# Holding all later zero fills of the GpSimd queue behind the FFN loads, and 42 instead of 50 up front

## Chip, cores, metric

One core of one Trainium2 chip. The metric is the device time of one execution in microseconds. All runs quoted here were fast. Ratios are computed as the mean time of one kernel's fast runs over that of the other's of the same rounds on the same chip, so they are not quite the ratios of the medians quoted beside them.

## The reference

A decode step (one token) of a transformer block: layernorm, attention of 16 query heads over 8 cached key and value heads, layernorm, a gated bilinear FFN; then all gradients of it. Only the last 4096 of the 32768 cache positions take part, so of the gradients of the two caches 7/8 are zero, and they must be written all the same:

```python
W = min(4096, max(256, Sk // 4))                       # 4096 of Sk = 32768
k = jnp.repeat(k_cache[:, :, Sk - W:, :], rep, axis=1)
v = jnp.repeat(v_cache[:, :, Sk - W:, :], rep, axis=1)
...
h2 = h + _B_ref(_layernorm(h), B_w_gate, B_w_up, B_w_down)
_out, _vjp = jax.vjp(_f, A_x, A_k_cache, A_v_cache, A_wq, A_wo, B_w_gate, B_w_up, B_w_down)
_grads = _vjp(grad_out)        # gradients of both caches: (1, 8, 32768, 256), bf16
```

## The kernel before

The zeros are written by 112 DMA transfers ("fills") of 2 MB each, all from one zeroed SBUF region, in rows of 16 KB (128 partitions x 8192 bf16). They are spread over three places: the GpSimd queue takes most, the SyncE queue takes 3 at each of five points around the FFN, and the last `NLATE` run on SyncE after everything else.

```python
ZW = 8192
NPRE = 50
NLATE = 9
fills = [zero_rows(o, g, 0, NZ, ZW)[i] for g in range(G) for o in (out_2, out_3) for i in range(NZ)]

def fill(eng, n):
    for _ in range(n):
        last = tc.keep_in_program_order(eng.dma_start(out=fills.pop(0), in_=zeros))
    return last

fill(ZQ, NPRE)                     # ZQ = GpSimd queue: the fills "up front"
# [... attention over 8 cache heads; their K and V are loaded on SyncE and ScalarE queues ...]
            elif g == 6:
                load_kv(V_at[7], A_v_cache, 7)
                load_wo(27, 32)
                fill(LD, 3)        # LD = SyncE queue
        load_wo(0, 19)
        load_ffn(*FB[0])
        fill(LD, 3)
# [... FFN, four rounds over the weights ...]
        for q, (f0, nw) in enumerate(FB):
            if q:
                load_ffn(f0, nw)   # w_down, w_gate, w_up; rows of 1 KB in w_gate and w_up
                fill(LD, 3)
            # [... compute; the next round's loads reuse this round's buffers ...]
        rest = fills[:-NLATE]
        for i, f in enumerate(rest):
            ins = ZQ.dma_start(out=f, in_=zeros)
            if i == 0:
                tc.add_manual_dep(ins.ins ..., ffn_last[0].ins.name, ..., reason="loads first")
# [... backward: 8 heads; each stores 2 x 2 MB through 3 staging buffers, and most also
#      weight-gradient "jobs" through 2 buffers, all on the SyncE queue ...]
            for o_ap, st_ in ((out_3, stV), (out_2, stK)):
                LD.dma_start(out=o_ap[0, g, Sk - W:, :].rearrange("(p t) d -> p t d", t=T), in_=st_)
            for job in plan[it]:
                job()
        for f in fills[-NLATE:]:
            tc.keep_in_program_order(LD.dma_start(out=f, in_=zeros))
```

Only the first fill of `rest` waits for the FFN loads, and without `keep_in_program_order` the scheduler may put the others in front of it.

Of the kernel before, what the change touches and what calls it, by code (L numbers as in the profile page):

```python
# [25 lines left out]
SCALE = 1.0 / 16.0  # L26
ZW = 8192
NZ = (Sk - W) * Dh // (128 * ZW)
NPRE = 50
NLATE = 9  # L30
KB = 512

# [2 lines left out]
def kernel(  # L35
# [5 lines left out]
    ZQ = nc.gpsimd  # L41
# [13 lines left out]
    def ar(off, n):  # L55
        return arena[:, off:off + n]
# [4 lines left out]
    zeros = ar(0, ZW)  # L61
# [67 lines left out]
    def fill(eng, n):  # L129
        last = None  # L130
# [4 lines that stand above are left out]
    fill(ZQ, NPRE)  # L135

# [244 lines left out]
    with tc.tile_pool(name="ps_mid", bufs=2, space=bass.MemoryType.PSUM) as ps_mid, \  # L381
# [61 lines left out]

        rest = fills[:-NLATE]
        for i, f in enumerate(rest):
            ins = ZQ.dma_start(out=f, in_=zeros)  # L446
            if i == 0:
                tc.add_manual_dep(ins.ins if hasattr(ins, "ins") else ins, ffn_last[0].ins.name, mybir.DependencyInfo(mybir.DependencyClass.Sync, mybir.DependencyReason.DATA), reason="loads first")

# [256 lines left out]
```

## Time and profile before

| | before |
|---|---|
| median of 4 runs | 838.37 us (837.80 to 838.44) |
| span of the profiled run | 836.3 us |
| bytes moved by DMA | 332.74 MB, 783 us at 425 GB/s |
| PE, VectorE, ScalarE busy | 55%, 44%, 24% |

The page of the kernel before has the busy tenths of the DMA engines and the rate they moved, in 40 slices of 20.9 us, and the DMA queues (q0 is the GpSimd queue, q1 SyncE, q10 ScalarE; packets, MB, share of the engines):

```profile
DMA  9999999999999999999999999999999987644699
GB/s 347 430 431 428 430 428 429 425 428 423 422 428 421 429 416 428 424 429 427 429 418 403 397 428 419 421 420 423 422 425 407 424 343 332 277 201 201 288 426 389
...
q0 software_dynamic: 12672, 184.56, 52.3%
q1 hardware_dynamic: 14758, 132.44, 38.1%
```

The DMA engines are full for 32 slices, then come six slices of a hole, then the nine late fills alone. A kernel bound like this can be read as a sum: the bytes at 425 GB/s, plus what the engines miss. The windows view of before, 20 us each (busy us of each engine with instruction counts, granted TensorE clock, DMA share, GB/s), shows the hole; it is 44 us of missed DMA. VectorE is the busiest compute engine in it:

```profile
core 0: us, PE busy (x) PEld busy (x) DVE busy (x) ACT busy (x) POOL busy (x), PEclk, DMA share, GB/s
660.00:680.00 20.00, 13.51 (x84) 6.00 (x83) 14.58 (x18) 7.43 (x12) 0.00 (x0) 0.69 1.00 423
680.00:700.00 20.00, 8.68 (x48) 4.02 (x49) 16.24 (x28) 6.24 (x11) 0.00 (x0) 0.66 0.76 302
...
740.00:760.00 20.00, 5.81 (x41) 1.85 (x41) 13.13 (x28) 9.26 (x17) 0.00 (x0) 0.52 0.47 197
...
780.00:800.00 20.00, 0.00 (x0) 0.00 (x0) 0.20 (x1) 0.03 (x1) 0.00 (x0) 0.50 0.99 419
```

The timeline of the GpSimd engine in before (start, duration, line; in brackets the idle time before it and what ended it) shows that the hold was not one. L132 is `fill`, L446 the loop over `rest`. Nine of these slip out before the held one goes at 468.63 us:

```profile
306.36 0.53 POOL L132 DMA_DIRECT2D out_dram<-arena  x1 [9.15 <-DMA out_dram<-arena]
312.66 0.53 POOL L446 DMA_DIRECT2D out_dram<-arena  x1 [5.78 <-DMA out_dram<-arena]
...
374.43 0.53 POOL L446 DMA_DIRECT2D out_dram<-arena  x1 [4.67 <-DMA out_dram<-arena]
468.63 4.18 POOL L446 DMA_DIRECT2D out_dram<-arena  x8 [93.68 <-DMA arena<-in_B_w_up_dram]
```

The chain of waits of before (start, duration, what) has the price of that: the first two FFN rounds wait 43 and 29 us for w_gate, the last two 10. A DMA piece of the chain runs from the issue of the transfer to its landing, so the engine behind it may have waited less (the waits view has 59.7 us of PE waiting for w_gate in all). The later lines are in the backward pass: VectorE, at the product of a weight-gradient job (L533), waits until one of the two job buffers is stored:

```profile
335.39 42.85 DMA arena<-in_B_w_gate_dram
...
402.70 28.73 DMA arena<-in_B_w_gate_dram
...
439.75 10.05 DMA arena<-in_B_w_gate_dram
...
457.52 9.71 DMA arena<-in_B_w_gate_dram
...
565.95 30.07 DMA out_dram<-arena
...
606.69 28.73 DMA out_dram<-arena
...
642.47 41.27 DMA out_dram<-arena
```

### The profile page before, as it was taken

To read this page: it belongs to the slowest core of one execution; us is meant where nothing else is said; L and a number is where in the kernel's file an instruction comes from. 1 tells how busy PE (TensorE), PEld (TensorE's weight loads), DVE (VectorE), ACT (ScalarE), POOL (GpSimd) and SP (SyncE) were. 2 spreads that over 40 slices of the span, in tenths; PEclk is the share of its full clock that TensorE was granted. 3 is DMA by queue.
4 is the path that set the end of the run, shared out by engine and by line. 5 is a ranking of instruction groups with operands and counts; after the bars stand their busy time and mean duration, and the time that the engine had idled before them with its cause. 6 is when DMAs were issued, how large, how long until landed. Compare 5 with 4: busy or idle time off the path is not lost.

```text
span 836.3 us, 8603 instructions
## 1 busy us (share of the span) xinstructions
PE 461.8 (55%) x3193; PEld 248.7 (30%) x3193; DVE 371.5 (44%) x1243; ACT 198.5 (24%) x325; POOL 51.9 (6%) x97
## 2 busy tenths in 40 slices
PE   0739999999994929041122319984534466542000
PEld 0414554554551505021011208542212232210000
DVE  2018256346240614020325490595746659965200
ACT  0322313323312000000000101572423143454100
POOL 4000010010010100010000201110000000000000
PEclk9969999999997969565555558996757666675555
DMA  9999999999999999999999999999999987644699
GB/s 347 430 431 428 430 428 429 425 428 423 422 428 421 429 416 428 424 429 427 429 418 403 397 428 419 421 420 423 422 425 407 424 343 332 277 201 201 288 426 389
DMA packets 28623, 332.74 MB, mean 398 GB/s; under 512 B 2979, under 2 KB 7206, under 8 KB 8742
## 3 DMA queue, kind: packets, MB, share of 16 engines
q0 software_dynamic: 12672, 184.56, 52.3%
q1 hardware_dynamic: 14758, 132.44, 38.1%
q10 hardware_dynamic: 1152, 15.20, 4.3%
q8 instruction: 25, 0.41, 0.2%
q14 instruction: 16, 0.13, 0.0%
HBM read 51.59 MB, written 280.59 MB: 397 GB/s over the span
## 4 chain that ended last, share of the span: by engine, by line
PE 39%; DMA 31%; DVE 13%; ACT 4%; another core or an unknown queue 4%; issue 1%; SPq 0%; DVEq 0%; ACTq 0%
DMA out_dram<-arena 13%; PE M_ps L334 13%; DMA arena<-in_B_w_gate_dram 11%; PE ok_ps L338 7%; PE rows_ps L274 7%; PE tr_ps L271 4%; DMA arena<-in_A_v_cache_dram 4%; DMA arena<-in_A_wq_dram 3%; DVE arena L649 3%; ACT arena L289 3%; DVE arena L650 2%; DVE arena L474 2%; PE d_ps L642 2%; PE dqb_ps L517 2%
## 5 line engine op out<-in xcount | busy, mean ns | idle before, releaser
L330 DVE TENSOR_SCALAR arena<-arena,p_f 128x256 bf16<-128x256 bf16 x512 | 110.0, 281 | 94.4 <-PE M_ps L334 94.4
L334 PE MATMUL M_ps<-arena 128*128 128x512 bf16 x512 | 125.3, 388 | 27.5 <-DMA arena<-in_A_v_cache_dram 27.5
L271 PE MATMUL tr_ps<-ident_bf,arena 128*128 128x128 bf16 x1024 | 90.5, 238 | 55.1 <-DMA arena<-in_A_k_cache_dram 31.0
L274 PE MATMUL rows_ps<-arena,vpad 128*16 128x512 bf16 x256 | 87.1, 438 | 30.2 <-DVE arena L606 22.0
L271 PEld LDWEIGHTS <-arena 128*128 128x128 bf16 x1024 | 67.7, 106 | 102.1 <-issue 50.9
L289 ACT COPY arena<-tr_ps 128x1024 bf16<-128x1024 bf16 x64 | 61.8, 1015 | 125.1 <-PE tr_ps L271 125.1
L642 PE MATMUL d_ps<-arena,rT 32*128 32x512 bf16 x256 | 40.2, 505 | 78.0 <-DVE arena L650 38.8
L334 PEld LDWEIGHTS <-arena 128*128 128x128 bf16 x512 | 46.9, 100 | 81.1 <-DMA arena<-in_A_v_cache_dram 28.0
L338 PE MATMUL ok_ps<-arena 128*16 128x256 bf16 x512 | 57.4, 273 | 0.9 <-DVE arena L316 0.9
L646 ACT CAST arena<-d_ps 128x512 bf16<-128x512 f32 x64 | 37.7, 590 | 67.5 <-PE d_ps L642 66.8
L650 DVE CAST arena<-d_ps 128x512 bf16<-128x512 f32 x64 | 43.5, 680 | 21.5 <-DMA out_dram<-arena 21.4
L649 DVE CAST arena<-d_ps 128x512 bf16<-128x512 f32 x64 | 43.9, 685 | 19.4 <-PE d_ps L642 19.3
L647 ACT CAST arena<-d_ps 128x512 bf16<-128x512 f32 x64 | 38.2, 596 | 48.7 <-DMA out_dram<-arena 48.7
L338 PEld LDWEIGHTS <-arena 128*16 128x16 bf16 x512 | 45.4, 90 | 13.9 <-issue 3.4
L423 PE MATMUL gu_ps<-X_b,arena 128*128 128x1 bf16 x84 | 7.2, 179 | 73.2 <-DMA arena<-in_B_w_gate_dram 59.7
L132 POOL DMA_DIRECT2D out_dram<-arena x50 | 27.1, 543 | 274.6 <-DMA out_dram<-arena 274.6
L604 ACT COPY arena<-tr_ps 128x1024 bf16<-128x1024 bf16 x32 | 32.7, 1021 | 42.2 <-DVE doX_f L474 23.5
L642 PEld LDWEIGHTS <-rT 32*128 32x128 bf16 x256 | 10.2, 95 | 100.4 <-issue 53.3
L274 PEld LDWEIGHTS <-vpad 128*16 128x16 bf16 x256 | 19.1, 91 | 64.2 <-issue 50.6
L446 POOL DMA_DIRECT2D out_dram<-arena x38 | 20.2, 532 | 282.4 <-DMA out_dram<-arena 188.8
L193 ACT CAST arena<-bc_ps 128x256 bf16<-128x256 f32 (+1 forms) x32 | 11.1, 347 | 107.1 <-PE bc_ps L192 105.9
L416 DVE CUSTOM_DVE_ANT_0 arena<-arena,dh_bc 128x448 bf16<-128x448 bf16 x14 | 8.8, 625 | 61.2 <-DMA arena<-in_B_w_down_dram 60.8
(193 smaller groups left out, 403.4 us busy)
## 6 DMA issues: line engine op xcount, KB each, us to landing
out_dram<-arena POOLq DMA_DIRECT2D x88, 2048.0 KB, 50.7
out_dram<-arena SPq DMA_DIRECT2D x40, 2048.0 KB, 19.9
arena<-in_A_k_cache_dram SPq DMA_DIRECT2D x7, 2048.0 KB, 15.1
arena<-in_A_v_cache_dram ACTq DMA_DIRECT2D x6, 2048.0 KB, 31.8
arena<-in_A_wq_dram SPq DMA_DIRECT2D x2, 3072.0 KB, 23.7
arena<-in_A_v_cache_dram SPq DMA_DIRECT2D x3, 2048.0 KB, 15.9
out_dram<-arena SPq DMA_DIRECT2D x3, 1344.0 KB, 22.1
out_dram<-arena SPq DMA_DIRECT2D x3, 1024.0 KB, 12.6
```

What stands on the lines that cost most here:

```text
L271: nc.tensor.transpose(tr_ps[:, dh, i, :], X_sb[:, 4 * q + i, dh * 128:(dh + 1) * 128], ident_bf[:])
L274: nc.tensor.matmul(rows_ps[:], lhsT=pad[:, dh, 16 * q:16 * q + 16], rhs=XT[:, dh].rearrange("p t k -> p (t k)"), start=(q == 0 and dh == 0 ...
L289: sT_ps = dots(K_at[g], KT_slot, vpad[g % 2], rows1, ps_c, "cols", lambda q, XT, ps: nc.scalar.copy(out=XT, in_=ps))
L330: nc.vector.tensor_scalar(out=pK[:, i, hh, :], in0=K_sb[:, t, :], scalar1=p_f[:, 8 * i + c, hh:hh + 1], scalar2=None, op0=ALU.mult)
L334: nc.tensor.matmul(M_ps[vh][:], lhsT=V_sb[:, t, vh * 128:(vh + 1) * 128], rhs=pK[:, i, :, :].rearrange("p h d -> p (h d)"), start=(t == 0) ...
L338: nc.tensor.matmul(ok_ps[:, k, :], lhsT=ppad[g % 2][:, 8 * (t % 4) + t // 4, :], rhs=X_sb[:, t, :], start=(g == 0 and k == 0 and t == 0), ...
L604: nc.scalar.copy(out=XT, in_=ps)
L642: nc.tensor.matmul(d_ps[:, qi].rearrange("p w d -> p (w d)"), lhsT=rT[32 * q:32 * (q + 1), :], rhs=RB_[32 * q:32 * (q + 1), l, :], start=T ...
L646: nc.scalar.copy(out=stV[:, t:t + 2, :], in_=d_ps[:, :, 0, :])
L647: nc.scalar.copy(out=stK[:, t:t + 2, :], in_=d_ps[:, :, 1, :])
L649: nc.vector.tensor_copy(out=stV[:, t:t + 2, :], in_=d_ps[:, :, 0, :])
L650: nc.vector.tensor_copy(out=stK[:, t:t + 2, :], in_=d_ps[:, :, 1, :])
```

## The change

The intent: clear the way for the FFN loads, and put the displaced fills where the hole is.

```diff
-NPRE = 50
+NPRE = 42
...
         for i, f in enumerate(rest):
-            ins = ZQ.dma_start(out=f, in_=zeros)
+            ins = tc.keep_in_program_order(ZQ.dma_start(out=f, in_=zeros))
             if i == 0:
                 tc.add_manual_dep(ins.ins ..., ffn_last[0].ins.name, ..., reason="loads first")
```

42 fills now go out up front and 46 stand behind the last FFN load.

## The prediction

> **What bounds the kernel now.** The DMA engines. The page: 332.74 MB, DMA digits 9 in the first 32 of 40 slices. In the table of 20 us windows they move 392 to 432 GB/s from 20 to 680 us, then only 302, 281, 197, 197 and 210 until 780, then about 425 for the nine zero fills that close the kernel. At 425 GB/s the bytes alone need 783 us. The hole from 680 to 780 us lacks 18.8 MB, 44 us; 783 + 44 + start and end give the span of 836. So only the hole, or new holes, can change the time. The Trainium skill (DMA: Bandwidth & Descriptors, Issuing engines are not separate DMA queues) says all queues share 16 engines; the trace agrees: GpSimd fills follow each other every 5 us alone, every 10 us beside SyncE transfers.
>
> **What the change does.** No work is added or removed; the other engines' instruction order stays. In before GpSimd issues 50 fills, and its timeline shows 9 more slip out from 313 to 374 us, ahead of the one held to 468.6 us; 29 follow there. After: 42, then 46 behind the last FFN load. 17 fills of 2.1 MB (35.7 MB, 84 us of DMA) move behind the FFN loads.
>
> **By stage.**
> 1. To about 306 us: the same (the 42nd fill lands there). V7's load, 15.9 us in the chain, gains 1 or 2 us.
> 2. About 308 to 332: only three SyncE fills are queued (15 us), PE still needs 24 us after V7 (chain). A new DMA gap of about 9 us.
> 3. FFN: the chain shows waits for w_gate of 42.9, 28.7, 10.1 and 9.7 us; the first two run beside GpSimd fills. The skill (same page, Queues, rings and completion order) says the engines switch between queues by packet, so small-row loads lose against 16 KB rows; the fills at full 5 us pace between 352 and 374 us, while the loads crawl, agree. Without fills all rounds take the 17 to 18 us of the last two (7.7 MB with three SyncE fills). The last FFN load should land near 397 us (380 to 410), not 468.6.
> 4. Backward: starts some 70 us earlier, its first cache-gradient stores at about 491, not 562. By then 16 of 46 fills are done, as in before. The other 30 (63 MB) share with 51.5 MB of SyncE traffic. In before such sharing (562 to 684) gave SyncE 201 GB/s and 37 to 53 us per head, against 20 to 25 without fills. Now it lasts for nearly all heads: last stores about 750 us, GpSimd fills to 755 to 775. The hole is mostly filled.
>
> Of 71 us gained in the FFN, most is given back by store waits. Balance: 836 - 44 (hole) + 9 (new gap) + 4 (FFN loops, DMA not quite full) + 3 (rest of a hole) = 808 span; the time runs 2 us longer.
>
> **Prediction: 810 us, range 797 to 827.** Faster by over 2%: 0.80; within 2%: 0.17; slower by over 2%: 0.03.
>
> **What would show it right.** GpSimd fills: 42, silence from about 260 to 397, then 46. First w_gate wait under 15 us, all FFN rounds near 18 us. DMA dips at 320 to 335 us. Store waits of 25 us or more until about 750 us; no window under 300 GB/s between 600 and 780. Matmul and VectorE busy times unchanged.
>
> **What would make it wrong.** FFN rounds limited by something else than bytes; fills draining well before the last heads, leaving a hole of 20 us or more; SyncE stores getting much less than half beside the fills, so that heads end after the fills and a compute tail remains; V7's load late.

## The result, and the profile after

The changed kernel took 828.31 us (median of 4 runs, 827.65 to 831.49), the kernel before 838.37: ratio 0.9889, 95% interval 0.9863 to 0.9915. It is 1.1% faster, where 3.4% was predicted, and lies just outside the stated range. The profiled run (831.49 us, span 829.7) was the slowest of the four, so its profile shows some 3 us more than the median.

The page of the changed kernel, same lines:

```profile
DMA  9999999999999994989999999999999999984799
GB/s 352 424 434 429 430 430 422 423 429 421 427 429 424 427 389 162 394 339 393 423 430 427 423 422 426 422 423 405 420 426 429 420 431 427 429 370 203 299 422 391
...
q0 software_dynamic: 12672, 184.56, 52.6%
q1 hardware_dynamic: 14758, 132.44, 38.7%
```

There is a new gap in the 16th slice and around it, and the late hole is shorter but not gone. The GpSimd timeline of the changed kernel shows the hold at work, and its chain of waits shows short FFN waits and a long series of store waits (the four below end again at weight-gradient jobs; four more, of 18, 17, 14 and 6 us, end at the copies into staging buffers):

```profile
260.47 0.53 POOL L132 DMA_DIRECT2D out_dram<-arena  x1 [8.62 <-DMA out_dram<-arena]
403.12 4.19 POOL L446 DMA_DIRECT2D out_dram<-arena  x8 [142.12 <-DMA arena<-in_B_w_up_dram]
```

```profile
391.51 10.21 DMA arena<-in_B_w_gate_dram
...
499.44 30.34 DMA out_dram<-arena
...
554.77 68.98 DMA out_dram<-arena x2
624.39 23.16 DMA out_dram<-arena
...
648.96 43.18 DMA out_dram<-arena
```

The last FFN load is in at 403 us instead of 469, 66 us sooner. But the last head's stores are issued at 774.06 us instead of 780.65. So 59 of the 66 us are handed back in the backward pass. The waits view says to whom; first the line of before, then that of the changed kernel (ScalarE at the copy into a staging buffer, waiting for its store: us in total, times, longest):

```profile
ACT arena L647 <- DMA out_dram<-arena: 48.7, 7, 13.5
```

```profile
ACT arena L647 <- DMA out_dram<-arena: 95.0, 7, 32.6
```

VectorE's waits for stores grew too: at its copy into a staging buffer (L650) from 21.4 to 50.7 us, at the weight-gradient products (L533) from 18.4 to 42.2. These waits overlap, so they don't add up.

### Why the store waits are long

The DMA view, limited to a window, counts packets and bytes by queue. One window of before, in which the FFN loads crawled (360 to 380 us):

```profile
q0 software_dynamic: 553, 8.03, 93.9%
q1 hardware_dynamic: 550, 0.53, 7.6%
```

The two queues moved the same number of packets, and 15 times the bytes went to the one with the long rows. The same two lines of the changed kernel, first at 535 to 555 us, where SyncE has mostly wide stores, then at 610 to 640 us, where the rows of out_8, of 3.5 and 1.8 KB, are among them:

```profile
q0 software_dynamic: 329, 4.72, 56.2%
q1 hardware_dynamic: 336, 3.77, 44.7%
```

```profile
q0 software_dynamic: 705, 10.26, 80.0%
q1 hardware_dynamic: 700, 2.53, 20.6%
```

In the second window, with packet counts equal again, SyncE has 2.53 MB in 30 us, 84 GB/s, and the stores of the heads queue behind its short rows.

A packet here is a row: 88 fills of 128 rows are 11,264, and 16 more for each fill make the 12,672 of q0 exactly. What these 16 are, no run here shows.

The Trainium skill (DMA: Bandwidth & Descriptors, Queues, rings and completion order) says that each engine takes turns between the queues packet by packet. The trace agrees, with 553 to 550, 705 to 700. So **while SyncE always has something to send and fills are there, each SyncE packet lets one fill packet pass.** The bytes of the rows, not a fair half, set the share.

### The profile page after: what moved, and what is told of

Its sections match the earlier page's. It is cut to its first block, busy times and chain, and to the rows that moved or that the text cites. A ratio compares the mean times of both kernels' runs of the same rounds, so it can differ in the third digit from the quotient of the medians.

```text
span 829.7 us, 8603 instructions
## 1 busy us (share of the span) xinstructions
PE 465.8 (56%) x3193; PEld 250.0 (30%) x3193; DVE 372.3 (45%) x1243; ACT 198.5 (24%) x325; POOL 53.0 (6%) x97
## 3 DMA queue, kind: packets, MB, share of 16 engines
q0 software_dynamic: 12672, 184.56, 52.6%
## 4 chain that ended last, share of the span: by engine, by line
PE 38%; DMA 37%; DVE 11%; ACT 4%; another core or an unknown queue 2%; issue 1%; SPq 0%; DVEq 0%; ACTq 0%
DMA out_dram<-arena 27%; PE M_ps L334 13%; PE ok_ps L338 7%; PE rows_ps L274 5%; PE tr_ps L271 4%; DMA arena<-in_A_v_cache_dram 3%; DMA arena<-in_A_wq_dram 3%; ACT arena L289 3%; DVE arena L649 2%; DVE arena L474 2%; PE dqb_ps L517 2%; DVE arena L650 2%; DMA arena<-in_B_w_down_dram 2%; PE d_ps L642 1%; DMA arena<-in_B_w_gate_dram 1%
## 5 line engine op out<-in xcount | busy, mean ns | idle before, releaser
L642 PE MATMUL d_ps<-arena,rT 32*128 32x512 bf16 x256 | 42.4, 519 | 115.9 <-ACT arena L647 68.6
L650 DVE CAST arena<-d_ps 128x512 bf16<-128x512 f32 x64 | 43.6, 682 | 50.7 <-DMA out_dram<-arena 50.7
L649 DVE CAST arena<-d_ps 128x512 bf16<-128x512 f32 x64 | 44.0, 687 | 21.4 <-PE d_ps L642 21.1
L276 DVE COPY arena<-rows_ps 16x512 f32<-16x512 f32 x16 | 10.8, 676 | 30.0 <-PE rows_ps L274 29.8
```

Of the source, the lines that this page charges most:

```text
L642: nc.tensor.matmul(d_ps[:, qi].rearrange("p w d -> p (w d)"), lhsT=rT[32 * q:32 * (q + 1), :], rhs=RB_[32 * q:32 * (q + 1), l, :], start=T ...
L649: nc.vector.tensor_copy(out=stV[:, t:t + 2, :], in_=d_ps[:, :, 0, :])
L650: nc.vector.tensor_copy(out=stK[:, t:t + 2, :], in_=d_ps[:, :, 1, :])
```

## The experiments

The table has what each kernel's DMA missed, counted from the windows view in 10 us windows as us of DMA at 425 GB/s. "Late" is 660 to 790 us (to 810 for the kernel marked \*, whose heads run on that long). Every kernel was run in 3 rounds beside the kernel before (medians of it 837.0 to 838.2 us). "Last head" is when the SyncE queue's last block of head stores is out and the late fills start to be issued.

| kernel | median us | ratio | FFN in | missed 300-480 | missed late | last head |
|---|---|---|---|---|---|---|
| before | 838.4 | 1 | 469 | 2 | 44 | 781 |
| changed | 828.3 | 0.9889 | 403 | 21 | 19 | 774 |
| e1 hold, 50 up front | 832.1 | 0.9932 | 427 | 6 | 37 | 776 |
| e2 no hold, 42 up front | 838.2 | 1.0007 | 469 | 3 | 44 | 781 |
| e3 changed, 2 late fills | 815.0 | 0.9727 | 404 | 20 | 0 | 783 |
| e4 changed, held fills in 8 KB rows | 818.6 | 0.9767 | 402 | 22 | 0 | 726 |
| e5 before, GpSimd fills in 4 KB rows | 814.0 | 0.9723 | 445 | 2 | 2 | 742 |
| e6 changed, GpSimd fills in 4 KB rows | 820.3 | 0.9797 | 397 | 10 | 3 | 695 |
| e7 changed, out_8 in long rows (wrong result) | 824.4 | 0.9847 | 402 | 20 | 13 | 766 |
| e8 before, 2 late fills | 832.3 | 0.9935 | 468 | 3 | 39\* | 810 |
| e9 before, GpSimd fills in 8 KB rows | 832.3 | 0.9933 | 470 | 1 | 35 | 775 |
| e10 e4 with 50 up front | 805.3 | 0.9606 | 427 | 6 | 7 | 748 |
| e11 e10 with 4 late fills | 802.9 | 0.9582 | 426 | 6 | 0 | 748 |

"FFN in" is the issue of the first held fill, which waits for the last FFN load.

My theory at the start: the time is bytes plus misses, and the packet turn explains the late miss. The rivals: the FFN gap alone cost the missing gain; the heads are bound by their own computation; queues share by bytes.

### e1: the hold alone

```diff
-NPRE = 42
+NPRE = 50
```

> Every later fill held, but 50 up front as in before. My theory (time is 783 us of bytes at 425 GB/s plus what the DMA engines miss: 21 us around the FFN and 20 us in a late hole in the changed kernel): the FFN loss falls from 21 to some 6 us, the last FFN load lands near 425 us, the late hole grows from 20 to some 32 us; time 822 to 832, level with the changed kernel. Rival (the FFN gap alone cost the missing gain, the late part follows along): about 813.

Measured: 832.13 us (830.55 to 833.27). The median lies at the upper end of the range (0.1 us above it). FFN in at 427 us, 6 us missed around it, 37 in the late hole. The rival falls: with the gap closed the time did not improve. Gap and hole traded almost one for one, a little worse than I expected for the hole. Within the change, 42 instead of 50 is worth some 0.4% on top of the hold (0.9889 against 0.9932; their intervals just overlap, so this is not clear of the noise).

### e2: the number alone

```diff
+NPRE = 42          # on the kernel before, hold unchanged
```

> 42 up front, only one later fill held. In program order 16 fills stand ahead of the held one, so 58 instead of 59 go out before the FFN loads are done. My theory: the number alone does nothing, 836 to 840 us, w_gate waits of 40 and 28 us as in before. Rival (the number does the work): under 832.

Measured: 838.21 us, ratio 1.0007 (0.9990 to 1.0024). As expected: where fills can slip past the hold, the number up front is only a label.

### e3: seven more fills on GpSimd, fewer at the end

```diff
-NLATE = 9
+NLATE = 2
```

> The changed kernel with 2 instead of 9 fills left for the end of the SyncE queue; 53 held ones on GpSimd. My theory: the late hole (20 us) is filled with the seven fills that otherwise run after the heads, the heads end later (near 800 instead of 773), the time is 808 to 814. Rival (fills beside the heads delay them one for one): 824 to 832.

Measured: 815.04 us (814.37 to 816.45), just above the range, ratio 0.9727. No late hole is left, and the heads end at 783 us, 9 us later, not 26. The hole was a place where the DMA could take work.

### e4: held fills in shorter rows

```diff
+    def short_rows(f, a):
+        return f.rearrange("p f -> (p f)").rearrange("(a p f) -> p a f", a=a, p=128)
...
-            ins = tc.keep_in_program_order(ZQ.dma_start(out=f, in_=zeros))
+            ins = tc.keep_in_program_order(ZQ.dma_start(out=short_rows(f, 2), in_=zeros.rearrange("p (a f) -> p a f", a=2)))
```

> The changed kernel with the held fills written in rows of 8 KB instead of 16 KB, same bytes, same result. My theory (the engines serve the two queues packet for packet, so the packet size sets the share): SyncE gets more than the 166 GB/s of the changed kernel between the first stores and the end of the fills, about 230; store waits of 30 us fall to about 20; the heads end some 10 to 20 us earlier, the fills later, the late hole falls below 8 us; time 810 to 816. Rival (queues share by bytes, or the heads are bound by their own computation): no change, 824 to 832.

Measured: 818.61 us (815.88 to 819.63), ratio 0.9767; a little above the range. The DMA view of e4 at 535 to 555 us, the window shown for the changed kernel:

```profile
q1 hardware_dynamic: 429, 5.19, 61.5%
q0 software_dynamic: 427, 3.27, 39.2%
```

The packet counts are equal again (429 and 427), and the shares have turned round: SyncE moves 5.19 MB instead of 3.77. From 495 to 700 us it had 41.7 MB, 204 GB/s (changed kernel: 33.3 MB, 162); I had expected about 230. The first store wait fell from 30.3 to 23.1 us. The last head came 48 us sooner, which is more than the 10 to 20 I expected, and the hole is gone. Nothing but the row length of the fills (and with it the order of addresses within one) was touched. Sharing by bytes and heads bound by computation both fall.

### e5: shorter rows alone, no better hold

```diff
+    # kernel before; all GpSimd fills through short_rows(f, 4), rows of 4 KB
```

> The kernel before (50 up front, one fill held, 9 slip out), with all GpSimd fills in rows of 4 KB. Packet theory: the w_gate waits of 42.9 and 28.7 us fall to under 20 each without any hold, the cache loads that wait 16 us beside fills fall to about 8, the last FFN load lands between 395 and 430 us with no dip under 350 GB/s before it, store waits fall to under 20 us, no late hole; 790 to 806 us. Rival (the FFN rounds need the fills out of the way, whatever their rows): 830 or more, w_gate waits over 30 us.

Measured: 814.00 us (813.08 to 815.73), ratio 0.9723: better than the change under study, without any change to its hold, but 8 us above my range. The four waits for FFN weights are 21, 23, 23 and 22 us where I expected under 20, and the last FFN load is in at 445 us where I expected 395 to 430; store waits fell to 11 to 14 us, and there is no late hole. The cache loads that wait 16 us fell to 14 only, not to 8. What I had not counted: the 4 KB rows themselves are slower. In most slices of the first 300 us the engines moved 405 to 417 GB/s, and 8.5 us are missed there after the first 10, where before missed none.

### e6: the changed kernel with 4 KB rows

```diff
+    # changed kernel; all GpSimd fills through short_rows(f, 4)
```

> The changed kernel with all GpSimd fills in rows of 4 KB. Packet theory: heads end earlier still than with 8 KB, no late hole, but the gap before the FFN stays or grows (the hold leaves nothing to write there): 21 to 30 us missed between 300 and 480 us; 810 to 818 us, slower than the kernel before with the same rows. Rival: better than the kernel before with the same rows.

Measured: 820.26 us, above the range, and slower than e5, as expected. The gap before the FFN is 10 us, not 21 to 30: with short rows the up-front fills had been held back themselves and lasted longer (5 MB of them moved from 300 to 340 us). The heads end at 695 us, far ahead of the fills; the DMA is full to the end but at the lower rate. Once the DMA is full, finishing the heads earlier buys nothing.

### e7: one store in longer rows

```diff
-LD.dma_start(out=out_8[0:1536, :].rearrange("(b p w) n -> p b (w n)", b=3, w=4), in_=buf[:, 0:12 * D].rearrange("p (b n) -> p b n", b=3))
+LD.dma_start(out=out_8[0:1536, :].rearrange("(p j) n -> p (j n)", j=12), in_=buf[:, 0:12 * D])
```

> The changed kernel with the first 1536 rows of out_8 stored in 128 rows of 10.75 KB instead of 384 of 3.5 KB (same bytes, the values land in the wrong order on purpose, so out_8 is wrong). Packet theory: 256 fewer packets, 16 per engine, each of which lets one 16 KB fill packet of some 0.6 us pass: the wait of 69 us around it falls by about 10, the fourth head's stores go out near 623 instead of 633 us, the hole shrinks from 20 to some 10 us; 815 to 822 us. Rival (bytes or computation set the pace of the heads): 825 to 831.

Measured: 824.43 us (823.66 to 825.85), ratio 0.9847; out_8 is wrong, as meant. 256 packets fewer of a single 1.4 MB store moved the next head's stores from 693.6 to 683.8 us, just the 10 us of the estimate, though one head later than I said (the short wait after it fell from 23.2 to 14.5 us). From 610 to 640 us the packet counts are equal again (606 of SyncE, 608 of the fills), and SyncE has 3.96 MB instead of 2.53. The hole shrank from 19 to 13 us and not to 10. The time is above my range and only 0.6 us below the rival's, so the time alone does not decide; the moved stores do, as the rival had them unmoved. So the direction and the size of the packet effect hold on the SyncE side too. The last head came 8 us sooner, and some 4 us of the 10 reached the end (ratios 0.9847 and 0.9889, with intervals that just overlap).

### e8: late fills moved, in the kernel before

```diff
-NLATE = 9
+NLATE = 2          # on the kernel before
```

> The kernel before with 2 instead of 9 fills left for the end of the SyncE queue, nothing else. Sum theory: seven fills, 34 us of DMA, go into the hole of 45 us; FFN as in before; 802 to 810 us, faster than the changed kernel with the same two. Rival (the gain needs the hold): 820 or more.

Measured: 832.25 us, ratio 0.9935. My expectation fails by 22 us. The same seven fills gained 13 us in the changed kernel and 5 in this one. The DMA view at 684 to 740 us, first of before, then of e8:

```profile
q1 hardware_dynamic: 1477, 14.71, 64.1%
```

```profile
q0 software_dynamic: 855, 12.30, 51.7%
q1 hardware_dynamic: 1339, 10.31, 43.6%
```

In before SyncE was alone there and moved 14.71 MB. In e8 the seven fills came just then, and it moved 10.31. The last head slipped from 781 to 810 us, 29 of the 34 us that seven fills take, and the hole behind it stayed. So the sum of bytes and misses is a good account but not a forecast: fills that meet a backlogged SyncE queue delay it nearly one for one, and fills that meet heads bound by their own computation cost less (in e3 the last head slipped by 9 of the 34 us). In the changed kernel the fills last to about 740 us, so that seven more fall on the last two heads, which need some 20 us each (in the chain of before 14 us of computation and 6 us for one store).

### e9: 8 KB rows in the kernel before

```diff
+    # kernel before; all GpSimd fills through short_rows(f, 2)
```

> The kernel before with all GpSimd fills in rows of 8 KB. The 4 KB rows gave 814 us, with 27 us of DMA missed, 12 of them because the engines moved 405 to 415 GB/s instead of 425 to 430 in the first 300 us. Theory: 8 KB rows keep 420 or more, the last FFN load lands between 440 and 465, a late hole of up to 12 us returns; 803 to 815 us. Rival (4 KB was needed to free the FFN loads): 820 or more.

Measured: 832.33 us; the rival was right. The first three FFN waits are 32, 36 and 35 us and the FFN is in at 470 us, no better than before. The turns are even again (340 to 360 us: 930 packets of the fills, 935 of SyncE), but against 1 KB rows the 8 KB packets still take most of the bytes, 7.17 MB to 1.32, and the slipped fills are still in the way. The heads run faster, but only to meet an empty queue: the hole is 35 us.

### e10 and e11: the hold, 50 up front, and short rows for the held fills

```diff
 # e4 with
-NPRE = 42
+NPRE = 50
 # e11 also
-NLATE = 9
+NLATE = 4
```

> Hold with 50 up front, held fills in rows of 8 KB. Theory: the FFN part misses 6 us as with the hold and 50 up front alone, the late hole falls from 37 us there to 8 to 20; heads end near 740 to 755 us; 803 to 815 us. Rival (the gap and the hole trade one for one, as 42 against 50 did with 16 KB rows): 817 or more.

> The same with 4 instead of 9 fills left for the end of the SyncE queue. Theory: the five moved fills run in the late hole, beside heads that are bound by their own computation; 796 to 806 us. Rival (fills beside heads delay them one for one, as in the kernel before with 2 left): no more than 3 us below the run with 9 left.

Measured: e10 805.33 us (803.30 to 806.10), ratio 0.9606; e11 802.90 us (802.13 to 803.67), ratio 0.9582, correct, and the fastest kernel. e10 is in its range: 6 us missed around the FFN, 7 late. Gap and hole no longer trade, because short rows let the heads end at 748 us, while fills are still there. The five fills moved in e11 did not delay the heads (748 in both), so nothing was traded one for one, but they gained only 2.4 us, since little hole was left. By its number (no more than 3 us) the rival is therefore not excluded; the heads that did not move speak against it. The page of e11:

```profile
DMA  8999999999999999999999999999999999999997
GB/s 344 430 432 429 429 427 425 426 429 426 428 425 426 429 412 427 431 422 403 385 402 398 418 413 414 416 422 413 422 403 424 409 428 430 425 423 423 426 423 312
```

Apart from the ends, no slice is below 385 GB/s. What remains above the 783 us of bytes is a few us each around the FFN, beside the heads, and at start and end.

## Why the prediction was wrong, point by point

- **DMA bounds the kernel; 17 fills move behind the FFN loads; 42, silence, 46.** Right: the counts are as stated, the silence runs from 260 to 403 us.
- **The last FFN load near 397 us (380 to 410).** Right: 403. w_gate waits about 10 us.
- **A new gap of 9 us, and 4 us in the FFN loops.** Mis-sized: 21 us missed from 300 to 480, 19 more than before, where the sum had 13. About 14 of them are from 310 to 340 us.
- **"Now it lasts for nearly all heads: last stores about 750 us, GpSimd fills to 755 to 775. The hole is mostly filled."** This is the step that failed. The last stores were issued at 774 us, and the fills ended first: q0 carried 63.5 MB between 495 and 743 us, which is all but 0.1 MB of what it had left. The term "+ 3 (rest of a hole)" measured 19 us.
- **The reason.** I had taken one rate, 201 GB/s for SyncE beside fills, from 562 to 684 us of before and stretched it over all heads. First, it was counted from issued bytes; the engines moved 23.07 MB there, 189 GB/s. Second, the window reached past the fills, which ran out between 670 and 680 us: from 562 to 670 us SyncE had 181 GB/s, and in the matching stretch of the changed kernel (495 to 603) 179. So far the sharing was as in before. Third, a share of bytes is no property of a queue. It follows the row length of what is in the queue, and the heads that now ran beside fills are those whose jobs store short rows. In before these rows had gone out almost alone (670 to 684 us: 3.47 MB, 248 GB/s):

```profile
q1 hardware_dynamic: 743, 3.47, 59.9%
q0 software_dynamic: 110, 1.52, 25.6%
```

In the changed kernel, rows of the same mean length met the fills (603 to 640 us: 3.85 MB, 104 GB/s):

```profile
q0 software_dynamic: 824, 11.98, 75.7%
q1 hardware_dynamic: 818, 3.85, 25.1%
```

Between 495 and 743 us SyncE got 41.3 MB, 167 GB/s, where the prediction had 201. I had quoted the packet rule for the FFN loads and named a SyncE share far below half as a risk, but did not apply the rule to the stores. e4 shows the packet cause on the fills' side, e7 on the stores' side.
- **The sum.** 836 - 44 + 19 (rest of the hole) + 19 (gap and FFN) = 830, the profiled span. With the two terms at their measured size, the accounting closes, as it must, since both were counted in that trace. That the terms pull on each other (e1, e8) is what it can't say.

What stays open: why the gap before the FFN lasted longer than the 9 us of the sum was not tested by a run of its own. Nor was it tested why only some 4 of e7's 10 us arrived.

## What to carry to other kernels

When two DMA queues compete, compare the row lengths in both before you assume how they share: bulk filler in long rows starves short-row loads and stores, and cutting the filler's rows is a priority knob that needs no synchronization, as long as the rows don't get so short that the rate falls (here 4 KB cost some per cent, 8 KB little), and short enough for what they compete with (8 KB did not help loads in 1 KB rows, e9). Background traffic is free only where the other queue leaves the engines idle; elsewhere it delayed the foreground nearly one for one here (e8, 29 of 34 us), so that what the hold gained early was largely paid back late. And a hold on one of many unordered instructions holds nothing but itself.

## What the Trainium skill lacked or had wrong

- DMA: Bandwidth & Descriptors (SWDGE vs HWDGE vs iDMA) puts a packet at "≤4096 B preferably". Here a packet was a whole row, of 16 KB in the fills: 12,672 packets for 184.56 MB; with 46 fills in 8 KB rows the total rose by 5,888, which is 46 x 128.
- The same page (Queues, rings and completion order) has the turn by packets, but not what follows for shares: 553 against 550 packets in 20 us were 8.03 against 0.53 MB.
- The same page (Specifications) names 512 B as the least transfer for full rate. From 420 to 475 us, with the fills nearly alone, rows of 16 KB moved 427 GB/s (changed kernel), of 8 KB 421 (e4), of 4 KB 403 (e6).
- The same page (Specifications) lists an HBM limit of about 358 GB/s for a core; this core, alone, wrote and read at 420 to 434 GB/s for most of the span. The page's section on bandwidth does say that a core alone reaches 425; the trace agrees with that.
